# A new order of operations and loads for an attention and mixer kernel

## The chip, the cores and the metric

The kernel runs on one core of one Trainium2 chip. The metric is the device time of one execution in microseconds, as the median of several runs. A core has five engines that run their own instruction streams in order and wait for each other by semaphores: TensorE (PE in the profile; its weight loads are listed apart as PEld), VectorE (DVE), ScalarE (ACT), GpSimd (POOL) and SyncE (SP). Matmul results go to PSUM, which has eight banks here of 128 partitions x 512 floats. POOL issues all loads that change float32 into bfloat16; SP issues stores and transposes by transfer.

## The reference

Eight batches of 576 positions; attention with 8 heads of 64, a causal window of 128 positions and a bias that falls off with distance; then a mixer with two small networks, over positions and over channels:

```python
scores = scale * np.matmul(q, k.transpose(0, 1, 3, 2))
scores = np.where(mask, scores + bias[None], -1e9)      # mask: 0 <= i - j < 128
attn = softmax(scores);  x = attn @ v                   # heads side by side: 8 x 576 x 512
h = np.maximum(x.transpose(0, 2, 1) @ w_tok1, 0.0) @ w_tok2      # 576 -> 256 -> 576
u = x + h.transpose(0, 2, 1)
return u + np.maximum(u @ w_ch1, 0.0) @ w_ch2                    # 512 -> 1536 -> 512
```

Inputs and output are float32; the kernel computes in bfloat16 with float32 sums.

## The kernel before, in words

Batches go in pairs. A pair has nine blocks of 128 positions: four of the even batch (0 to 3), four of the odd one (4 to 7), and block 8, called the tail, which holds the last 64 positions of both batches. The window of 128 means that a block needs the keys and values of itself and of the block before it alone.

For each block the steps are these, with their lines. Load q, k and v (line 518, POOL). Transpose q and k on PE (638) and copy them out of PSUM (644, DVE or ACT); from the tenth block on a transpose by transfer on SP does it (627). Scores (678, PE; two blocks of the first batch, 0 and 1, add the bias on PE in 687). Exponential (701, ACT). Multiplication by the mask (711, DVE; not in blocks 0 and 1). Values (745, PE). Division by the sum (758 and 761, DVE, or 767, ACT). When a batch's blocks are there: the first token matrix (790, then 800 for the last 64 positions), a ReLU (808 or 809), the second token matrix (833, 829 for the tail), the addition (851, or in the first batch 836 on PE and 848 on ACT), and a transposition of the result (868 on PE and 874, or from batch 2 on by transfer, 859). Then the channel network: first matrix (1015, 1030, 1073 for the tail, 952 in the last batch), ReLU (1036, 1078), second matrix (1218, 1118, 1247), with seven products of halves in place of eight, whose sums of operands DVE makes (576 and 594 for weights, 1055 for activations). DVE adds the result (1186), and it is stored.

While PE works on the channel network of a batch, the attention of the next batch is woven in between. At the start there is no such work, so the first batch's attention is a bare chain.

The order of all this is not written out. A planner in the kernel's own Python (class `Plan`, lines 66 to 314) takes every operation with an engine, a cost in ns, a rank and its dependencies, and builds the order of each engine by simulating them at build time: of the operations that could start first, the one with the lowest rank goes. It also has a model of the loads: when the stream of loads begins (`START`), how long each occupies it (packets times `PACKET`), and how long after that its data is there (`LATE`, with a second value for loads issued after `FETCH`). `CASTS` says when the first four float32 tiles are there. POOL issues the loads in the order of the list `LOADS`; at most eight are out at a time. A load of q or k also needs a free buffer of five, and so the transposes of the block that had it before.

In `LOADS`, q2 means q of block 2, and so on; W1 and W2 are the token matrices (P1 a second copy of W1's last rows, T0 the last columns of W2), A0 to A3 are quarters of the first channel matrix (three of its twelve column groups each), and B0 to B3 quarters of the second. Blocks 0 and 3 of q and k are not in the list: they come as float32 by SP and ACT (line 481) and are cast (533).

Where the plan has a gap on PE in the first 60 us, `emit` puts filler matmuls on a tile of zeros (line 1302) there, as long as the planned gap, so that PE is never without work for long. They are fixed instructions: they run whether or not the gap is there.

The random numbers: each part of the program (the first batch's attention, then each batch) had a seed, and each of its operations' ranks was moved by a random amount of up to 1500 ns (`SHIFT`); a seed of 0 leaves a part alone.

Of the kernel before, what the change touches and what calls it, by code (L numbers as in the profile page):

```python
# [3 lines left out]

# [58 lines left out]
    pass  # L63


class Plan:
    def __init__(self):
        self.rings, self.ops, self.orders, self.part = {}, [], 0, 0

    def ring(self, name, slots, pair=None):  # L70
        self.rings[name] = Ring(slots, pair)
# [4 lines left out]
    def op(self, eng, cost, emit, rank, makes=(), adds=(), part=None, uses=(), reads=(), needs=(),  # L76
           after=0.0, order=None, bus=0.0, other=None, mode=0, behind=()):
        def many(x):
            return list(x) if isinstance(x, (list, tuple)) else [x]

        o = Op()
        o.eng, o.cost, o.emit, o.rank, o.after, o.part = eng, cost, emit, rank, after, self.part
        o.t0 = o.done = None
        o.order, o.bus, o.other, o.mode = order, bus, other, mode
        o.n = len(self.ops)
        o.deps = set(many(needs))
        o.behind = list(behind)
# [29 lines left out]

    def run(self):
        ops = self.ops
        dice = [random.Random(x) for x in SEEDS]  # L120
        for o in ops:
            if SEEDS[o.part]:
                o.rank += dice[o.part].uniform(-SHIFT, SHIFT)
        succ = {o: [] for o in ops}
        left, held = {}, []
        ready = {o: o.after for o in ops}
# [21 lines left out]
        todo = len(ops)  # L148
        lines, coming, clock, flying = ([], []), [], START, 0

# [55 lines left out]
        while todo:  # L206
# [94 lines left out]
    def emit(self, spin):  # L301
# [11 lines left out]
        for _, _, go in sorted(work, key=lambda w: w[:2]):  # L313
# [20 lines left out]
RANKH = 0  # L334
RELU = 350
SUMS_AT = 60e3
SEEDS = [45795, 495947, 190309, 331881, 0, 67117, 67408, 179769, 445757]
SHIFT = 1500.0
UNIT_LATE = False
SECOND_LATE = True  # L340
BIASED = [0, 1]
THIRD = [(4, 5)]
# [7 lines left out]
DENSE = 20000.0  # L350
CHILLY = 7400.0
MORE = 150.0
START = 3900.0
RAW = 3
CASTS = [4800.0, 5400.0, 6000.0, 6000.0]
PACKET = 0.813
LATE = (2400.0, 2790.0)
FETCH = 9500.0
STORE = 774.0
TURN = [(792.0, 1267.0), (1380.0, 2400.0)]  # L360
RATES = [(0.37, 0.23), (0.52, 0.35), (0.47, 0.18)]
# [1 line left out]
EARLY = 1  # L363


LOADS = ("q2 k2 k1 q1 v0 W2 k8 q8 v2 v1 v3 v8 W1 q7 k7 A0 P1 k5 q5 k4 v5 "
         "q4 A1 v4 k6 q6 A2 v7 v6 A3 T0 B0 B1 B2 B3")


@with_exitstack  # L370
def kernel(
# [16 lines left out]
    P = nc.NUM_PARTITIONS  # L388
    B, H, S, D = q.shape
# [4 lines left out]
    NC = S // P  # L394
    R = S - NC * P
# [5 lines left out]
    NHT = DCH // P  # L401
# [12 lines left out]
    plan = Plan()  # L414
# [106 lines left out]
    def weights(parts):  # L521
        return [plan.dma(lambda o=o, i=i: nc.gpsimd.dma_start(out=o, in_=i), n, s) for o, i, n, s in parts]

    w1 = moe_w_tok1[0 : NC * P, :].rearrange("(c p) n -> p c n", p=P)
    w2 = moe_w_tok2.rearrange("(j p) s -> p j s", p=P)
    c1 = moe_w_ch1.rearrange("(j p) h -> p j h", p=P)
    c2 = moe_w_ch2.rearrange("(j p) c -> p j c", p=P)

    for i_, raw in enumerate(raws):
        buf, i = block(0, (0, RAW)[i_ // 2])["qk"], i_ % 2  # L530

        def cast(eng=dve_.tensor_copy, raw=raw, buf=buf, i=i):
            eng(out=buf()[:, i, :, :], in_=raw.rearrange("p (h d) -> p h d", h=H))

        plan.op("DVE", (520, 660)[i], cast, -100 + i_, makes=buf, after=CASTS[i_],
                **({"other": ("ACT", 600, lambda cast=cast: cast(act_.copy))} if i_ > 1 else {}))
    if PADT:
        for i in range(2):
            plan.op("DVE", 190, lambda i=i: dve_.memset(W1p[(1 - i) * R : (2 - i) * R, i, :], 0.0), -90)
    lw1, lw2, lw2t, lc1, lc2 = [], [], [], [], []  # L540
    for item in LOADS.split():
        what, n = item[:-1], int(item[-1])
        if what in ("q", "k", "v"):
            load(what, 0, n, parts_of(0, n))
        elif what == "W":
            if n == 1:
                lw1 += weights([(W1[:, 0:NC, :], w1, 512, 2080)] +
                               [(W1p[0:R, 0, :], moe_w_tok1[NC * P : S, :], 64, 210)])
            else:
                lw2 += weights([(W2[:, :, :], w2[:, :, 0 : NC * P], 256, 2630)])  # L550
        elif what == "P":
            lw1 += weights([(W1p[R:P, 1, :], moe_w_tok1[NC * P : S, :], 64, 210)])
        elif what == "T":
            lw2t += weights([(W2t[:, :, :], w2[:, :, NC * P : S], 256, 300)])
        elif what == "A":
            hs = slice(n * DCH // 4, (n + 1) * DCH // 4)
            lc1 += weights([(WC1[:, :, hs], c1[:, :, hs], 512, 2500)]) * (NHT // 4)
        else:
            js = slice(n * NHT // 4, (n + 1) * NHT // 4)
            lc2 += weights([(WC2[:, js, :], c2[:, js, :], 384, 2680)]) * (NHT // 4)  # L560
    for pr in range(1, B // 2):
        for blk in sum(turns_of(pr), []):
            for name in "qkv":
# [358 lines left out]
    def unit(b, u, rank, uT, tt, r2):  # L922
# [23 lines left out]
        def product(m, bk, more=(), new=True):  # L946
            l, r, ws, ts = L[m]

            def go():
                for c in range(2):  # L950
                    for cb in range(2):
# [192 lines left out]
    def second(b, rank, r2, ss, sums, ub):  # L1144
        pr, half = b // 2, b % 2
        final = b == B - 1
        g1, g2, g3 = bank(ANY), bank(TWO if final else ANY), bank(ANY)
        obs = {}
        capt = {}

# [22 lines left out]
        def both(bk):  # L1173
            return bk().rearrange("p (c n) -> p c n", c=2)[:, :, 0:HN]

        def evict(m, bk, row, col, last):
            key = (row, col)
            blks = [half * NC + 2 * row, half * NC + 2 * row + 1]
            cols = slice(col * HN, (col + 1) * HN)
            old = obs.get(key)  # L1180
            ob = old or obs.setdefault(key, plan.buf("ob"))

            def go():
                v = ob().rearrange("p (c n) -> p c n", c=2)
                src = v if old else ub()[:, blks[0] : blks[0] + 2, cols]
                dve_.tensor_tensor(out=v, in0=both(bk), in1=src, op=ALU.add)  # L1186

            rk = rank(0)
# [12 lines left out]
            if late:  # L1201
                plan.dma(store, 2 * P, -1, uses=ob)
            else:
                plan.op("SP", 550, store, rk, uses=[ob])

        DONE = {1: (0, 0, False), 5: (1, 1, False), 6: (0, 1, False), 7: (1, 1, True), 2: (0, 0, True), 3: (0, 1, True), 4: (1, 0, True)}
        for m in PRODUCTS:
# [5 lines left out]
            for g in range(2):  # L1213
# [60 lines left out]
    side(0, along(-1e6, 1.0, 1.0))  # L1274
    for b in range(B):
        n = LEN[b % 2]
        plan.part = b + 1
        marks["wait"] = []
        main(b, along(base, n, n))
        wait = marks["wait"]  # L1280
        if b + 1 < B:
            nb = b + 1
            tot = SIDE[nb // 2 >= HALVED][nb % 2] + 8 * 216 + 216 + (5 if nb % 2 else 4) * (656 if nb < FROM_U else 432)
            if nb > 1:
                tot -= 450 * sum(by_transfer(nb // 2, x) for x in turns_of(nb // 2)[nb % 2])
# [52 lines left out]
```

## Time and profile before

| What | Value |
|---|---|
| Median of 3 runs | 279.0 us (278.68, 279.0, 279.62) |
| Profiled execution, span from first to last instruction | 277.5 us |
| What lies around the span, median less span | 1.5 us |
| Granted TensorE clock | 0.999 |
| Bytes moved by DMA | 38.71 MB, mean 139 GB/s |

The profile is of one execution. A line of a timeline has the start and the length in us, then engine, line of the kernel, operation, output and inputs, and how many instructions are merged in it; in brackets is idle time of the engine just before, and what ended it. In a group the numbers behind the bar are busy time and the mean length of one in ns, then the idle time before. A matmul's length holds its way through the queue, so matmuls overlap, and starts tell more than lengths. A load's row has its size and the time from issue to landing.

### The profile page before, as it was taken

The numbers are of one execution on the slowest core, as the hardware profiler recorded it, in microseconds if no ns is written. First come the engines' busy times: TensorE is split into PE (matmuls) and PEld (weight loads), VectorE is DVE, ScalarE is ACT, GpSimd is POOL, SyncE is SP. The second block draws the span as 40 slices with busy tenths as digits, with TensorE's granted clock in tenths as the row PEclk, the third lists the DMA queues.
The fourth block names the chain that finished last, engine by engine and source line by source line (L and its number), as shares of the span: only waits on it lengthen the run. The fifth ranks groups of instructions, "written<-read, shape, count | busy, mean of one in ns | idle before, by whom it ended". The sixth has DMA issues, their size and how long they took to land.

```text
span 277.5 us, 7005 instructions
## 1 busy us (share of the span) xinstructions
PE 269.9 (97%) x2827; PEld 180.1 (65%) x2827; DVE 209.6 (76%) x497; ACT 139.8 (50%) x238; POOL 114.0 (41%) x144
## 2 busy tenths in 40 slices
PE   7899999999999999999999999999999999999994
PEld 3565765685686555595567655576667645689883
DVE  6577699978897569853989478763989549877983
ACT  5573894336960298207951096206860079105650
POOL 8889865940256037900585009600472220013000
PEclk9999999999999999999999999999999999999999
DMA  8999999999699999999899989999499750043014
GB/s 155 163 159 160 183 194 186 155 133 218 107 113 105 177 234 140 131 135 185 175 134 143 196 214 97 138 155 246 50 120 99 197 140 0 2 127 121 1 57 135
DMA packets 167553, 38.71 MB, mean 139 GB/s; under 512 B 155808, under 2 KB 166688, under 8 KB 167520
## 3 DMA queue, kind: packets, MB, share of 16 engines
q0 software_dynamic: 114032, 19.77, 92.1%
q1 hardware_dynamic: 51264, 17.83, 33.4%
q10 hardware_dynamic: 2224, 0.66, 1.2%
q8 instruction: 22, 0.36, 0.5%
q14 instruction: 11, 0.09, 0.1%
HBM read 35.85 MB, written 9.44 MB: 163 GB/s over the span
## 4 chain that ended last, share of the span: by engine, by line
PE 93%; DMA 2%; DVE 2%; ACT 1%; issue 0%; SPq 0%; DVEq 0%
PE ps L1218 26%; PE ps L1030 25%; PE ps L745 7%; PE ps L678 6%; PE ps L790 5%; PE ps L833 5%; PE ps L1073 4%; PE ps L1118 4%; PE ps L952 3%; DMA raw<-in_q_dram 2%; PE ps L1302 2%; PE ps L638 2%; PE ps L800 1%; PE ps L829 1%; PE ps L868 1%; PE ps L1015 1%
## 5 line engine op out<-in xcount | busy, mean ns | idle before, releaser
L1030 PE MATMUL ps<-uT,WC 128*128 128x512 bf16 x328 | 79.1, 379 | 0.4 <-DVE xb L761 0.4
L701 ACT ACTIVATE pe<-ps 128x1024 bf16<-128x1024 f32 (+1 forms) x76 | 63.5, 889 | 27.0 <-PE ps L678 25.7
L518 POOL DMA_DIRECT2D v<-in_v_dram x40 | 34.1, 857 | 92.7 <-PE ps L745 89.2
L1036 ACT ACTIVATE r<-ps 128x512 bf16<-128x512 f32 x75 | 44.4, 602 | 40.5 <-PE ps L1030 38.5
L1030 PEld LDWEIGHTS <-WC 128*128 128x128 bf16 x328 | 29.3, 98 | 30.1 <-issue 1.3
L711 DVE TENSOR_TENSOR pe<-pe,mask 128x1024 bf16<-128x1024 bf16 (+1 forms) x64 | 38.1, 608 | 7.2 <-ACT pe L701 6.8
L1218 PEld LDWEIGHTS <-r 128*128 128x128 bf16 x372 | 35.9, 98 | 7.2 <-issue 0.2
L518 POOL DMA_DIRECT2D qk<-in_k_dram x38 | 32.8, 870 | 3.6 <-DMA v<-in_v_dram 1.6
L518 POOL DMA_DIRECT2D qk<-in_q_dram x38 | 32.8, 868 | 2.7 <-DMA WC<-in_moe_w_ch_dram 1.0
L1218 PEld LDWEIGHTS <-s 128*128 128x128 bf16 x288 | 27.5, 98 | 6.0 <-issue 1.3
L761 DVE TENSOR_TENSOR xb<-ps,rt 128x256 bf16<-128x256 f32 (+1 forms) x72 | 29.2, 416 | 0.7
L745 PEld LDWEIGHTS <-pe 128*128 128x128 bf16 (+1 forms) x560 | 22.3, 98 | 8.7 <-DVE pe L711 2.2
L745 PE MATMUL ps<-v,pe 128*128 128x65 bf16 (+1 forms) x560 | 26.2, 194 | 0.2 <-DVE pe L711 0.2
L1218 PE MATMUL ps<-WC,r 128*128 128x256 bf16 x192 | 25.4, 273 | 0.0
L1218 PE MATMUL ps<-WT,s 128*128 128x256 bf16 x192 | 24.6, 273 | 0.0
L851 DVE TENSOR_TENSOR ub<-ps,xb 128x512 bf16<-128x512 f32 x34 | 21.2, 681 | 1.8 <-PE ps L833 1.8
L1218 PE MATMUL ps<-WT,r 128*128 128x256 bf16 x180 | 22.4, 272 | 0.0
L678 PEld LDWEIGHTS <-qkT 64*128 64x128 bf16 x560 | 14.7, 94 | 11.1 <-issue 9.4
L1186 DVE TENSOR_TENSOR raw<-ps,ub 128x512 f32<-128x512 f32 x21 | 14.3, 685 | 9.1 <-PE ps L1218 8.9
L678 PE MATMUL ps<-qkT 64*128 64x128 bf16 (+1 forms) x304 | 19.4, 216 | 0.0
L1078 ACT ACTIVATE r2t<-ps 128x512 bf16<-128x512 f32 x12 | 7.2, 603 | 22.5 <-PE ps L1073 22.5
L758 DVE RECIPROCAL rt<-ps 128x4 f32<-128x4 f32 (+1 forms) x76 | 12.4, 174 | 6.8 <-PE ps L745 6.3
(105 smaller groups left out, 350.7 us busy)
## 6 DMA issues: line engine op xcount, KB each, us to landing
out_dram<-raw SPq DMA_DIRECT2D x17, 256.0 KB, 2.6
v<-in_v_dram POOLq DMA_DIRECT2D x32, 128.0 KB, 5.4
qk<-in_q_dram POOLq DMA_DIRECT2D x30, 128.0 KB, 5.6
qk<-in_k_dram POOLq DMA_DIRECT2D x30, 128.0 KB, 5.4
WC<-in_moe_w_ch_dram POOLq DMA_DIRECT2D x8, 384.0 KB, 9.1
out_dram<-ob SPq DMA_DIRECT2D x6, 256.0 KB, 2.6
out_dram<-ob POOLq DMA_DIRECT2D x4, 256.0 KB, 3.1
out_dram<-raw POOLq DMA_DIRECT2D x4, 256.0 KB, 2.9
```

The source lines that it names most:

```text
L518: nc.gpsimd.dma_start(out=to()[p0 : p0 + n, :, :], in_=rows(src, b, s0, n))
L678: pe_.matmul(wide(e)[:, i, kind, a:z], lhsT=ts[kb]()[e * D : (e + 1) * D, NHP + i, :], rhs=ts[blk]()[e * D : (e + 1) * D, i, a:z], start=n ...
L701: act_.activation(out=pb()[:, e, :, lo:, c0:c1_], in_=wide(e)[:, :, lo:, c0:c1_], func=ACT.Exp, scale=scale)
L711: dve_.tensor_tensor(out=o, in0=o, in1=heads(mk, es), op=ALU.mult)
L745: pe_.matmul(view()[a:z, at, i, :], lhsT=pb()[:, e, i, kind, a:z], rhs=vb()[:, h, 0 : D + 1], start=m == 0, stop=m == len(mms) - 1, skip_g ...
L761: dve_.tensor_tensor(out=x4(), in0=view()[r0:r1_, :, :, 0:D], in1=rt()[r0:r1_, 0:n, :, :].broadcast_to([r1_ - r0, n, 4, D]), op=ALU.mult)
L790: pe_.matmul(t1[j]()[:, :], lhsT=W1[:, c, j * P : (j + 1) * P], rhs=xb()[:, blk, :], start=c == 0, stop=False)
L851: plan.op("DVE", 690, lambda blk=blk, ht=ht, hs=hs: dve_.tensor_tensor(out=ub()[:, blk, :], in0=ht()[:, hs], in1=xb()[:, blk, :], op=ALU.a ...
L1030: pe_.matmul(ct()[:, :], lhsT=WC1[:, cb, t * P : (t + 1) * P], rhs=uT()[:, cb, :], start=cb == 0, stop=cb == NCB - 1)
L1036: plan.op("ACT", 600, lambda t=t, ct=ct: act_.activation(out=r2()[:, t, :], in_=ct()[:, :], func=ACT.Relu), rk, part=(r2, t), uses=[ct], o ...
L1186: dve_.tensor_tensor(out=v, in0=both(bk), in1=src, op=ALU.add)
L1218: pe_.matmul(of(bk, c), lhsT=l(t, c), rhs=w(t), start=first, stop=g == 1 and t == HK - 1, skip_group_check=True)
```

## The change

Four things change together, all in what the planner is given.

The model of the first transfers is set to other values: the stream of loads begins 1300 ns later, loads issued after 9.0 us land 3500 ns after their place in the stream instead of 2790 (after 9.5 us), the float32 tiles are there at 5.0, 5.68, 7.56 and 8.04 us, and W1, W2 and the quarters B are given fewer packets. The list of loads has another order. Since A, B and W1's parts no longer come in the order in which they are numbered, the lists of weights (`lw1`, `lc1`, `lc2`) are filled by place. The random shifts come from a hash instead of a generator, and there are now seeds for groups of 30 operations, and of two parts for each batch (its channel network, and the next batch's attention and token mixing).

Two new constants, `EV` and `GONE`, stand at values that change nothing. No operation is added or removed, but the planner may give a copy to another engine and makes other fillers. Some fifteen lines are added ahead of most of the program, so a line such as 833 is 848 in the changed kernel; the text uses the old numbers, and calls the same line there its twin.

```diff
+def offset(o):
+    seed = SEEDS.get(o.group, 0)
+    z, full = (seed << 20) + o.part * 1000 + o.at, (1 << 64) - 1
+    z = (z + 0x9E3779B97F4A7C15) & full
+    z = ((z ^ (z >> 30)) * 0xBF58476D1CE4E5B9) & full
+    z = ((z ^ (z >> 27)) * 0x94D049BB133111EB) & full
+    return ((z ^ (z >> 31)) >> 11) * 2.0**-52 - 1.0 if seed else 0.0
...
+        o.at = self.inside.get(self.part, 0)
+        self.inside[self.part] = o.at + 1
+        o.group = self.part * 10 + min(o.at // GROUP, 9)
...
-        dice = [random.Random(x) for x in SEEDS]
         for o in ops:
-            if SEEDS[o.part]:
-                o.rank += dice[o.part].uniform(-SHIFT, SHIFT)
+            o.rank += SHIFT * offset(o)
...
-SEEDS = [45795, 495947, 190309, 331881, 0, 67117, 67408, 179769, 445757]
+SEEDS = {0: 846071, 4: 412855, 5: 343328, 6: 901394, 7: 671959, 8: 764867, 10: 416701, 11: 351752, 12: 70309, 20: 619675, 21: 120696, 22: 577973, 23: 405716, 30: 213057, 31: 165847, 32: 71954, 40: 404590, 41: 482568, 50: 286568, 51: 611926, 60: 579527, 61: 819459, 62: 379002, 70: 640395, 71: 934419, 72: 439456, 80: 109511, 81: 910233, 82: 748762, 90: 519950, 91: 197367, 101: 150347, 102: 405724, 110: 7956, 111: 36992, 112: 363882, 120: 129293, 122: 874736, 130: 359970, 131: 803027, 140: 23914, 141: 388902, 142: 496852, 150: 220523, 151: 220010, 152: 75231, 153: 900190}
+GROUP = 30
 SHIFT = 1500.0
+EV = 0.0
+GONE = False
...
-START = 3900.0
+START = 5200.0
-CASTS = [4800.0, 5400.0, 6000.0, 6000.0]
+CASTS = [5000.0, 5680.0, 7560.0, 8040.0]
-LATE = (2400.0, 2790.0)
-FETCH = 9500.0
+LATE = (2400.0, 3500.0)
+FETCH = 9000.0
...
-LOADS = ("q2 k2 k1 q1 v0 W2 k8 q8 v2 v1 v3 v8 W1 q7 k7 A0 P1 k5 q5 k4 v5 "
-         "q4 A1 v4 k6 q6 A2 v7 v6 A3 T0 B0 B1 B2 B3")
+LOADS = ("k1 q1 k2 q2 v0 k8 q8 v1 v2 v8 v3 W1 q7 q4 k4 W2 q6 "
+         "k6 A0 k7 q5 A3 k5 v7 v4 A1 v6 v5 A2 B0 T0 P1 B2 B1 B3")
...
-                lw1 += weights([(W1[:, 0:NC, :], w1, 512, 2080)] +
+                lw1[0:2] = weights([(W1[:, 0:NC, :], w1, 512, 1670)] +
...
-                lw2 += weights([(W2[:, :, :], w2[:, :, 0 : NC * P], 256, 2630)])
+                lw2 += weights([(W2[:, :, :], w2[:, :, 0 : NC * P], 256, 1520)])
...
-            lc2 += weights([(WC2[:, js, :], c2[:, js, :], 384, 2680)]) * (NHT // 4)
+            lc2[n * NHT // 4 : (n + 1) * NHT // 4] = weights([(WC2[:, js, :], c2[:, js, :], 384, 2400)]) * (NHT // 4)
...
-        plan.part = b + 1
+        plan.part = 2 * b + 1
...
+            plan.part = 2 * b + 2
```

More of the change, by code (lines that the diff above doesn't have):

```diff
@@ L2 @@
 import math
-import random
 import concourse.bass as bass
@@ L63 @@
     pass
+def offset(o):
[5 more added lines that the diff above has]
+    return ((z ^ (z >> 31)) >> 11) * 2.0**-52 - 1.0 if seed else 0.0
 class Plan:
     def __init__(self):
-        self.rings, self.ops, self.orders, self.part = {}, [], 0, 0
+        self.rings, self.ops, self.orders, self.part, self.inside = {}, [], 0, 0, {}
     def ring(self, name, slots, pair=None):
@@ L539 @@
             plan.op("DVE", 190, lambda i=i: dve_.memset(W1p[(1 - i) * R : (2 - i) * R, i, :], 0.0), -90)
-    lw1, lw2, lw2t, lc1, lc2 = [], [], [], [], []
+    lw1, lw2, lw2t, lc1, lc2 = [None] * 3, [], [], [None] * NHT, [None] * NHT
+    plan.items = []
     for item in LOADS.split():
         what, n = item[:-1], int(item[-1])
+        first = len(plan.ops)
         if what in ("q", "k", "v"):
@@ L546 @@
             if n == 1:
-                lw1 += weights([(W1[:, 0:NC, :], w1, 512, 2080)] +
+                lw1[0:2] = weights([(W1[:, 0:NC, :], w1, 512, 1670)] +
                                [(W1p[0:R, 0, :], moe_w_tok1[NC * P : S, :], 64, 210)])
             else:
-                lw2 += weights([(W2[:, :, :], w2[:, :, 0 : NC * P], 256, 2630)])
+                lw2 += weights([(W2[:, :, :], w2[:, :, 0 : NC * P], 256, 1520)])
         elif what == "P":
-            lw1 += weights([(W1p[R:P, 1, :], moe_w_tok1[NC * P : S, :], 64, 210)])
+            lw1[2:3] = weights([(W1p[R:P, 1, :], moe_w_tok1[NC * P : S, :], 64, 210)])
         elif what == "T":
@@ L556 @@
             hs = slice(n * DCH // 4, (n + 1) * DCH // 4)
-            lc1 += weights([(WC1[:, :, hs], c1[:, :, hs], 512, 2500)]) * (NHT // 4)
+            lc1[n * NHT // 4 : (n + 1) * NHT // 4] = weights([(WC1[:, :, hs], c1[:, :, hs], 512, 2500)]) * (NHT // 4)
         else:
             js = slice(n * NHT // 4, (n + 1) * NHT // 4)
-            lc2 += weights([(WC2[:, js, :], c2[:, js, :], 384, 2680)]) * (NHT // 4)
+            lc2[n * NHT // 4 : (n + 1) * NHT // 4] = weights([(WC2[:, js, :], c2[:, js, :], 384, 2400)]) * (NHT // 4)
+        plan.items.append(plan.ops[first:])
     for pr in range(1, B // 2):
@@ L1146, in second @@
         final = b == B - 1
-        g1, g2, g3 = bank(ANY), bank(TWO if final else ANY), bank(ANY)
+        SB = ANY if final or not GONE else ONE
+        g1, g2, g3 = bank(SB), bank(TWO if final else SB), bank(SB)
         obs = {}
@@ L1186, in go @@
                 dve_.tensor_tensor(out=v, in0=both(bk), in1=src, op=ALU.add)
-            rk = rank(0)
+            rk = rank(0) - EV
             kw = {"adds": ob} if old else {"makes": ob, "reads": [(ub, x) for x in blks]}
```

## The prediction

> **What bounds the kernel now.** I read the page first, then PE's waits, then PE, DVE, ACT and the loads in order of time for the first 30 us.
>
> ```profile
> span 277.5 us, 7005 instructions
> PE 269.9 (97%) x2827; PEld 180.1 (65%) x2827; DVE 209.6 (76%) x497; ACT 139.8 (50%) x238; POOL 114.0 (41%) x144
> PE 93%; DMA 2%; DVE 2%; ACT 1%; issue 0%; SPq 0%; DVEq 0%
> ```
>
> Span, busy time, and the engine shares of the chain that ended last: PE holds 93% of it. So time can only come from PE's work, from its waits, or from what PE does that is no work. The last is there:
>
> ```profile
> L1302 PE MATMUL ps<-zero 128*128 128x452 bf16 (+10 forms) x45 | 11.8, 381 | 1.0 <-DVE zero L482 1.0
> PE ps L638 <- DVE qk L533: 2.0, 3, 1.3
> PE ps L1030 <- DVE xb L761: 0.4, 1, 0.4
> PE ps L745 <- DVE pe L711: 0.2, 1, 0.2
> 50.00:100.00 50.00, 50.00 (x512) 33.39 (x510) 40.02 (x93) 24.17 (x42) 18.34 (x23) 1.00 1.54 149
> 200.00:250.00 50.00, 50.00 (x512) 33.12 (x510) 38.39 (x83) 20.24 (x33) 11.81 (x16) 1.00 0.73 97
> ```
>
> A group of matmuls (busy, mean), PE's waits (us, times, longest), two stretches (length, then busy PE, PEld, DVE, ACT, POOL, granted clock, DMA share, GB/s). The 45 filler matmuls (line 1302) all stand before 25 us; PE is busy with them for up to 11.8 us, a union of overlapping spans that counts their queues double. After 30 us PE waits for 0.6 us in all, and in the late stretches for nothing. Hence the first 25 us are the only place with something to gain, and any wait set up later is a loss.
>
> ```profile
> 6.23 0.40 PE L638 MATMUL ps<-ident,qk 128*128 128x128 bf16 x4 [0.19 <-DVE qk L533]
> 8.31 0.78 PE L638 MATMUL ps<-ident,qk 128*128 128x128 bf16 x8 [1.34 <-DVE qk L533]
> 9.02 0.40 PE L678 MATMUL ps<-qkT 64*128 64x128 bf16 x8
> 11.10 0.23 PE L678 MATMUL ps<-qkT 64*128 64x128 bf16 x2
> 14.05 1.25 PE L1302 MATMUL ps<-zero 128*128 128x508 bf16 x5
> 21.22 0.68 PE L745 MATMUL ps<-v,pe 128*128 128x65 bf16 x16
> 21.82 1.90 PE L790 MATMUL ps<-xb,W 128*128 128x512 bf16 x8
> 23.65 0.60 PE L800 MATMUL ps<-xb,W1p 64*128 64x512 bf16 x2
> 24.98 1.46 PE L833 MATMUL ps<-r,W 128*128 128x512 bf16 x6
> 28.91 0.62 PE L1015 MATMUL ps<-uT,WC 128*128 128x128 bf16 x8
> ...
> 7.53 0.72 DVE L533 CAST qk<-raw 128x512 bf16<-128x512 f32 x1 [1.04 <-DMA raw<-in_q_dram]
> 8.17 0.41 DVE L644 COPY qkT<-ps 128x512 bf16<-128x512 bf16 x1
> 9.12 0.69 DVE L644 COPY qkT<-ps 128x1024 bf16<-128x1024 bf16 x1 [0.55 <-PE ps L638]
> ...
> 9.45 1.08 ACT L701 ACTIVATE pe<-ps 128x512 bf16<-128x512 f32 x2 [0.82 <-PE ps L678]
> 11.77 1.94 ACT L701 ACTIVATE pe<-ps 128x1024 bf16<-128x1024 f32 x2 [1.23 <-PE ps L678]
> 19.00 1.09 ACT L701 ACTIVATE pe<-ps 128x512 bf16<-128x512 f32 x2 [1.10 <-PE ps L745]
> ```
>
> PE, DVE, ACT in order of time (start, length, what). The first batch is a chain of small steps: transpose, copy, scores, exponential, mask, values, then the token weights at 21.82. DVE's second copy of block 0 (8.17) was ready when PE's transposes of 6.23 ended, but stood behind a cast whose input landed at 7.5.
>
> ```profile
> 1.37 1.03 POOL L518 DMA_DIRECT2D qk<-in_q_dram  x1 [0.30 <-issue]
> 5.01 0.91 POOL L518 DMA_DIRECT2D v<-in_v_dram  x1
> 5.87 0.74 POOL L522 DMA_DIRECT2D W<-in_moe_w_tok_dram  x1
> 14.69 0.79 POOL L522 DMA_DIRECT2D W<-in_moe_w_tok_dram  x1
> 17.87 0.88 POOL L518 DMA_DIRECT2D qk<-in_k_dram  x1 [0.94 <-DVE qkT L644]
> 18.74 0.77 POOL L522 DMA_DIRECT2D WC<-in_moe_w_ch_dram  x1
> 36.36 0.76 POOL L522 DMA_DIRECT2D WC<-in_moe_w_ch_dram  x1 [1.22 <-DMA WC<-in_moe_w_ch_dram]
> ...
> qk<-in_q_dram POOLq DMA_DIRECT2D x1, 128.0 KB, 7.1
> v<-in_v_dram POOLq DMA_DIRECT2D x1, 128.0 KB, 6.8
> W<-in_moe_w_tok_dram POOLq DMA_DIRECT2D x1, 256.0 KB, 7.2
> W<-in_moe_w_tok_dram POOLq DMA_DIRECT2D x1, 256.0 KB, 5.9
> qk<-in_k_dram POOLq DMA_DIRECT2D x1, 128.0 KB, 4.5
> WC<-in_moe_w_ch_dram POOLq DMA_DIRECT2D x1, 384.0 KB, 5.6
> WC<-in_moe_w_ch_dram POOLq DMA_DIRECT2D x1, 384.0 KB, 10.7
> ```
>
> Seven loads: when POOL issues each, and, in the same order, its time to landing. Sums: q2 (the first) lands at 8.5, v0 (the fifth) at 11.8, W2 at 13.1, W1 at 20.6, k7 at 22.4, A0 at 24.3, B3 (the last weight) at 47.1. So a load of 128 KB takes (11.8 - 8.5) / 4 = 0.83 us of the stream and W2 some 1.25. The stream is the pace-maker: what moves ahead in it moves all behind it back.
>
> **The change, part by part.** The engines together do the same real work in another order (some copies pass from DVE to ACT or back); the fillers are 42 of 17,868 columns instead of 45 of 18,712. Counted from the first token matmul, PE's columns and its changes between row groups come out alike in both orders, to under 0.05 us. So no gain or loss from PE's work itself: what counts is when the first token matmuls start, and waits behind.
>
> *Block 0.* DVE now does both copies of block 0 before the casts of block 3. Copy two starts when the transposes of 6.23 end (6.65) and takes 0.41; scores of block 0 at 7.1 instead of 9.02. In return both casts of block 3 are DVE's (one was ACT's): 0.72 from 7.53, then 0.6, until 8.85, and block 3's transposes move from 8.31 to 8.9. Nobody needs block 3 early now.
>
> *Load order k1 q1 k2 q2 v0.* Block 1 takes the two slots at 8.5 and 9.3. Its transposes follow block 3's at 9.4, its two bias groups (0.9 us) cover the two copies (0.69 each, DVE, 9.6 to 11.0), and its scores come at 11.0, where block 3's were (11.10). ACT then begins a full block at 11.65 against 11.77, no gain, but its next ones follow without the waits of before: block 2 (landed 10.9, scores at 13.0) 13.6 to 15.5, block 3 (scores at 14.8) 15.5 to 17.5, the tail block 17.5 to 18.6, against 19.00 to 20.09. That is 1.5 us earlier.
>
> *W2 moved behind q4 and k4.* All of k8, q8, v1, v2, v8, v3, W1 land 1.25 us earlier: W1 at 19.3, v3 before it at no later than 18.1. With scores of the tail block ending near 17.2, PE still has, in its new order: values of block 2 (0.5), three fillers (0.5), values of block 3 with two fillers between (0.7), two fillers (0.35), values of the tail with two fillers and two token matmuls between (1.2), six token matmuls (1.3): 4.55 us, so line 800's twin starts at 21.75 against 23.65. Inputs in time: v3 18.1 for a use at 18.2, the tail's masks near 19.1 for 19.3. Gain here 1.9; the bounds are 1.25 (the loads alone) and 2.3 (all waits gone).
>
> *What comes late next: W2.* From line 800 to line 833 the old order took 24.98 - 23.65 = 1.33 us; the new one would be there at 23.1. W2 now stands after all that k7 stood after, less k7, plus q4, k4: 22.4 + 0.83 = 23.2, with bounds 22.9 and 23.9 from the rounding of the rows and the size of the load. Waiting behind it on PE are all eight matmuls of line 833 and everything after. I take 23.4: 1.6 us gained.
>
> *A0 moved back by three loads* (q4, q6, k6 ahead of it and k4 for k7): 24.3 + 3 x 0.83 = 26.8. Line 1015 came 3.93 after line 833, so it would be at 27.35: covered, by 0.5. Next the transposes of block 7 need k7 at 26.8 + 0.83 = 27.65 for a use at 27.8: bare. A3, k5, v4 and v6 have some 0.5 each by the same count. I charge 0.2 for these together (0 to 0.6).
>
> *The last weights.* The set ahead of B3 is the same, so it lands near 47.1 again; the second product that reads it has moved back to about 53, its first neighbours read B0 and B2 alone. No wait. DVE's sums that read B3 (0.47 each, two) stand before the five additions of batch 1 and would be done near 48.1, the first addition is due near 49: cover 0.8.
>
> *After 50 us.* Ranks have new offsets in groups of 30 operations. Counted in columns at full clock, the distance in PE time from a block's scores to its values has, from batch 2 on, the same least values in both orders (1.9 and 2.1 us); from the last line 833 of a batch to its first line 1030 it is 6.1 us at least against 6.5 (batch 2), by transfer; where the old had no wait. Batch 1 alone is tighter, 3.1 against 4.2. I take 0, bounds -0.6 (its waits go) and +1.5. The last 45 matmuls and stores are alike: 0. Code that is added but switched off (`EV`, `GONE`) costs nothing.
>
> **Sum.** -1.6 + 0.2 + 0 = -1.4 us: span 276.1. The median of the runs lies 1.5 above the profiled span (279.0 against 277.5), so 277.6.
>
> [...]
>
> **Rivals.**
>
> *The landings take the gain back.* The order is drawn for the landings of another order. If v1 to v3, W2, A0 and k7 each come 0.5 late, line 833 starts at 23.9 and block 7 costs 0.5 more: 1.1 - 0.2 - 0.5 = 0.4 us gained, 278.6. For it: four uses with under 0.3 us of cover. Against: the stream's pace is steady at 0.83.
>
> *W2 late, slower.* W2 is now needed as soon as it lands; before it lay ready for 11.9 us (13.1 to 24.98). The point that decides is a landing at 25.0. If POOL may issue only when older loads have landed (the 1.22 us it sat before 36.36 shows such a wait), one missed place puts two loads' time and the wait on it: 23.4 + 1.7 + 0.9 = 26.0, all behind shifts 1.0, and A0 and k7 with it: 280.2. Against: its issue would be near 17.8, 5 us ahead.
>
> *A wait in batch 1 or later.* Batch 1's five additions stand in a row on DVE (0.62 each), then copies, and PE comes 1.1 us sooner: a wait of 1 to 1.5 there leaves 279.0.
>
> [...]
>
> **Chances.** Forecast (277.6; its own range 276.5 to 278.4) 0.6. Landings take it back 0.13 and a wait in batch 1 or later 0.09: both mostly within 0.3%. W2 late 0.16, clock 0.02. 0.3% is 0.84 us, about what a measurement of this kernel tells from no change. Faster 0.6, same 0.18, slower 0.22. Range: below, all waits gone, 1.9 + 0.6 = 2.5, 276.5; above, to W2 late, 280.2.
>
> **What would show it.** Right: line 678's twin at 7.1 for block 0, ACT's tail exponentials near 17.5, line 800's twin near 21.8, line 833's near 23.4, 1.5 us kept to the end. Wrong: a PE wait on W2 or A0 of over 1 us, new PE waits after 50 us, or ACT's second full block not following the first.

## The result, and the profile after

The changed kernel takes 277.38 us in the median (277.34 to 277.7), the kernel before 279.22 beside it: a ratio of 0.9945, 95% interval 0.993 to 0.9961. It is faster by 1.84 us; 277.6 was predicted. The median of the kernel before rests on four executions here; all 72 of it on record have 278.88, and against these the gain is 1.5 us, which is also what the ratio says (1.1 to 2.0). The profiled execution took 277.36, with a span of 275.6 against 277.5; the spans of 68 other executions of the kernel before have a median of 277.1. Three executions of the kernels in the experiments ran far longer than the others of the same kernel (284.87, 959.72 and 351.16 us), and medians and ratios are without them.

The page of the changed kernel: span, busy times, engine shares of the chain that ended last.

```profile
span 275.6 us, 6968 instructions
...
PE 268.4 (97%) x2790; PEld 180.8 (66%) x2824; DVE 210.3 (76%) x496; ACT 139.1 (50%) x239; POOL 114.0 (41%) x144
...
PE 81%; DMA 6%; DVE 5%; POOL 4%; issue 2%; SPq 1%; POOLq 0%
```

All waits of its PE (us, times, longest):

```profile
PE ps L1319 <- DVE zero L494: 1.0, 1, 1.0
PE ps L1045 <- DMA uT<-ub: 0.2, 1, 0.2
```

Its fillers (line 1302 is 1319 there), as a group with busy time and mean length behind the bar:

```profile
L1319 PE MATMUL ps<-zero 128*128 128x460 bf16 (+13 forms) x42 | 12.1, 401 | 1.0 <-DVE zero L494 1.0
```

Behind the start one wait of 0.2 us is left. The fillers are 42 as foreseen; of PE's 2824 matmuls 34 have no record in this trace. In the chain DMA, DVE and POOL now hold 15%: the loads themselves have become part of what sets the end. PE, then ACT and POOL of the changed kernel in order of time (start, length):

```profile
7.33 0.40 PE L693 MATMUL ps<-qkT 64*128 64x128 bf16 x8
9.51 1.04 PE L702 MATMUL ps<-WS 128*128 128x256 bf16 x8
10.61 0.23 PE L693 MATMUL ps<-qkT 64*128 64x128 bf16 x2
13.42 0.61 PE L653 MATMUL ps<-ident,qk 128*128 128x128 bf16 x8
21.68 0.60 PE L815 MATMUL ps<-xb,W1p 64*128 64x512 bf16 x2
23.01 0.59 PE L848 MATMUL ps<-r,W 128*128 128x512 bf16 x2
27.05 0.62 PE L1030 MATMUL ps<-uT,WC 128*128 128x128 bf16 x8
27.50 0.83 PE L653 MATMUL ps<-ident,qk 128*128 128x128 bf16 x8
...
11.27 1.94 ACT L716 ACTIVATE pe<-ps 128x1024 bf16<-128x1024 f32 x2 [2.43 <-PE ps L693]
13.39 4.83 ACT L716 ACTIVATE pe<-ps 128x1024 bf16<-128x1024 f32 x6 [0.18 <-PE ps L693]
...
13.47 0.78 POOL L534 DMA_DIRECT2D W<-in_moe_w_tok_dram  x1
17.42 0.74 POOL L534 DMA_DIRECT2D W<-in_moe_w_tok_dram  x1
19.89 0.81 POOL L534 DMA_DIRECT2D WC<-in_moe_w_ch_dram  x1
20.63 0.95 POOL L530 DMA_DIRECT2D qk<-in_k_dram  x1
```

The last four rows issue W1, W2, A0 and k7; the loads' own view has, in the same order, their time to landing:

```profile
W<-in_moe_w_tok_dram POOLq DMA_DIRECT2D x1, 256.0 KB, 5.3
W<-in_moe_w_tok_dram POOLq DMA_DIRECT2D x1, 256.0 KB, 5.5
WC<-in_moe_w_ch_dram POOLq DMA_DIRECT2D x1, 384.0 KB, 7.1
qk<-in_k_dram POOLq DMA_DIRECT2D x1, 128.0 KB, 7.3
```

W1 landed at 18.8 (20.6 before), W2 at 22.9, A0 at 27.0, k7 at 27.9. Line 815 starts at 21.68 (its twin 800 at 23.65), line 848 at 23.01 (833 at 24.98), line 1030 at 27.05 (1015 at 28.91). So the changed kernel is 1.97 us ahead at line 848, and it ends 1.9 ahead. From the first start of line 848 to the end of the span the changed kernel takes 275.6 - 23.01 = 252.6 us, the old kernel 277.5 - 24.98 = 252.5. The whole gain is made before 23 us and kept. W2 landed 0.09 us before it was used, A0 0.05.

### The profile page after: what moved, and what is told of

It is laid out like the page before. It is cut to its first block, busy times and chain, and to the rows that moved or that the text cites. A ratio compares the mean times of both kernels' runs of the same rounds, so it can differ in the third digit from the quotient of the medians.

```text
span 275.6 us, 6968 instructions
## 1 busy us (share of the span) xinstructions
PE 268.4 (97%) x2790; PEld 180.8 (66%) x2824; DVE 210.3 (76%) x496; ACT 139.1 (50%) x239; POOL 114.0 (41%) x144
## 4 chain that ended last, share of the span: by engine, by line
PE 81%; DMA 6%; DVE 5%; POOL 4%; issue 2%; SPq 1%; POOLq 0%
PE ps L1234 25%; PE ps L1045 24%; PE ps L760 6%; PE ps L693 5%; DMA qk<-in_k_dram 5%; PE ps L805 4%; PE ps L848 4%; PE ps L1088 4%; PE ps L967 3%; PE ps L1133 3%; DVE pe L726 2%; POOL qk L530 2%; POOL v L530 1%; DMA uT<-ub 1%; PE ps L815 1%
## 5 line engine op out<-in xcount | busy, mean ns | idle before, releaser
L1045 PE MATMUL ps<-uT,WC 128*128 128x512 bf16 x306 | 77.9, 379 | 1.3 <-DMA uT<-ub 0.2
L716 ACT ACTIVATE pe<-ps 128x1024 bf16<-128x1024 f32 (+1 forms) x76 | 63.4, 890 | 19.1 <-PE ps L693 18.8
L1051 ACT ACTIVATE r<-ps 128x512 bf16<-128x512 f32 x77 | 45.0, 604 | 51.4 <-PE ps L1045 49.3
L726 DVE TENSOR_TENSOR pe<-pe,mask 128x1024 bf16<-128x1024 bf16 (+1 forms) x64 | 38.7, 609 | 12.0 <-ACT pe L716 11.5
L760 PEld LDWEIGHTS <-pe 128*128 128x128 bf16 (+1 forms) x560 | 22.6, 98 | 9.1 <-DVE pe L726 1.3
L760 PE MATMUL ps<-v,pe 128*128 128x65 bf16 (+1 forms) x560 | 26.9, 194 | 0.3
L1202 DVE TENSOR_TENSOR raw<-ps,ub 128x512 f32<-128x512 f32 x22 | 15.0, 686 | 8.1 <-PE ps L1234 8.1
L1093 ACT ACTIVATE r2t<-ps 128x512 bf16<-128x512 f32 x12 | 7.2, 600 | 22.9 <-PE ps L1088 22.7
```

Of the source, the lines that this page charges most:

```text
L716: act_.activation(out=pb()[:, e, :, lo:, c0:c1_], in_=wide(e)[:, :, lo:, c0:c1_], func=ACT.Exp, scale=scale)
L726: dve_.tensor_tensor(out=o, in0=o, in1=heads(mk, es), op=ALU.mult)
L760: pe_.matmul(view()[a:z, at, i, :], lhsT=pb()[:, e, i, kind, a:z], rhs=vb()[:, h, 0 : D + 1], start=m == 0, stop=m == len(mms) - 1, skip_g ...
L1045: pe_.matmul(ct()[:, :], lhsT=WC1[:, cb, t * P : (t + 1) * P], rhs=uT()[:, cb, :], start=cb == 0, stop=cb == NCB - 1)
L1051: plan.op("ACT", 600, lambda t=t, ct=ct: act_.activation(out=r2()[:, t, :], in_=ct()[:, :], func=ACT.Relu), rk, part=(r2, t), uses=[ct], o ...
```

## The experiments

The theories at the start were these. Theory 1: the gain is the 1.25 us that W2 no longer takes from the loads ahead of it. Theory 2: it is the new model of the first transfers, which gives DVE another order at block 0 and fillers that fit. Theory 3: it is the new random offsets. The table has every kernel that ran: its median, the ratio with its interval to the kernel before, which ran beside each (medians 278.84 to 279.22), and, from the profile, the span, the first start of line 848 (or 833), and the difference of the two, here called the rest.

| Kernel | Median us | Ratio | Span | 848 | Rest |
|---|---|---|---|---|---|
| before | 278.8 to 279.2 | | 277.5 | 24.98 | 252.5 |
| changed | 277.38 | 0.9945 (0.993 to 0.9961) | 275.6 | 23.01 | 252.6 |
| loads alone | 279.15 | 1.0008 (0.9999 to 1.0017) | 277.7 | 24.38 | 253.3 |
| model alone | 287.63 | 1.0309 (1.0273 to 1.0345) | 287.2 | 24.32 | 262.9 |
| no offsets | 279.25 | 1.0007 (0.9993 to 1.0021) | 277.2 | 24.19 | 253.0 |
| old loads | 290.91 | 1.0437 (1.0405 to 1.0469) | 288.4 | 23.82 | 264.6 |
| W2 issued sixth | 278.66 | 0.9996 (0.9983 to 1.0009) | | 24.51 | |
| W2 issued later | 279.11 | 1.0021 (1.0 to 1.0043) | 277.5 | 24.57 | 252.9 |
| cast first | 277.54 | 0.9956 (0.9943 to 0.9969) | 275.8 | 23.84 | 252.0 |
| no fillers | 279.97 | 1.0042 (1.0027 to 1.0058) | 278.8 | 24.00 | 254.8 |
| start's offsets alone | 278.08 | 0.9964 (0.9943 to 0.9986) | 276.2 | 23.10 | 253.1 |
| later offsets alone | 278.66 | 0.999 (0.9969 to 1.0011) | 276.8 | 23.85 | 253.0 |
| fillers to 12 us | 278.91 | 0.9987 (0.996 to 1.0014) | 275.9 | 22.68 | 253.2 |
| other offsets | 290.25 | 1.038 (1.031 to 1.0451) | 286.8 | 23.98 | 262.8 |

### One part alone, or one part left out

*Loads alone*: the old kernel with the new list of loads (and its lists of weights filled by place, as in the change).

```diff
-LOADS = ("q2 k2 k1 q1 v0 W2 k8 q8 v2 v1 v3 v8 W1 q7 k7 A0 P1 k5 q5 k4 v5 "
-         "q4 A1 v4 k6 q6 A2 v7 v6 A3 T0 B0 B1 B2 B3")
+LOADS = ("k1 q1 k2 q2 v0 k8 q8 v1 v2 v8 v3 W1 q7 q4 k4 W2 q6 "
+         "k6 A0 k7 q5 A3 k5 v7 v4 A1 v6 v5 A2 B0 T0 P1 B2 B1 B3")
```

> The kernel before with the new list of loads alone: old values in the model of the transfers, old seeds. Theory 1 (the gain is W2's 1.25 us taken out of the way of the first batch's loads): most of the gain, 278.0, and line 790 near 20.6. Theory 2 (the gain is the model's: DVE's order at block 0 and fillers that fit): no gain, 279.2. Theory 3 (the gain is the new seeds): 279.2 too.

*Model alone*: the old kernel with the new values of the model.

```diff
-START = 3900.0
+START = 5200.0
-CASTS = [4800.0, 5400.0, 6000.0, 6000.0]
+CASTS = [5000.0, 5680.0, 7560.0, 8040.0]
-LATE = (2400.0, 2790.0)
-FETCH = 9500.0
+LATE = (2400.0, 3500.0)
+FETCH = 9000.0
...
-                lw2 += weights([(W2[:, :, :], w2[:, :, 0 : NC * P], 256, 2630)])
+                lw2 += weights([(W2[:, :, :], w2[:, :, 0 : NC * P], 256, 1520)])
```

(and W1's and the B quarters' values, as in the change)

> The kernel before with the new values of the model alone (START, CASTS, LATE, FETCH, packets of W1, W2 and B): old list of loads, old seeds. Theory 1: 279.2, since W2 still stands in the way. Theory 2: block 0's scores near 7.1 and 278.0. Theory 3: 279.2.

*No offsets*: the changed kernel without any random offset, its list of seeds empty.

```diff
+SEEDS = {}
```

> The changed kernel without any random shift of ranks. Theories 1 and 2: the start keeps its gain, 277.6 to 278.0, if the plain ranks make no new waits. Theory 3: the gain goes, 279.2 or more.

*Old loads*: the changed kernel with the list of loads of before (the first diff, reversed).

> The changed kernel with the old list of loads, planned anew for it: new model, new seeds. Theory 1: the first token matmuls come 1.25 us later than with the new list, 278.6. Theory 2: 277.6. Theory 3: 277.6.

No part holds the gain. At line 848 the loads alone are worth 0.6 us, the model alone 0.66, both without offsets 0.79, all three 1.97. What each gains at the start is lost again behind 25 us or nearly so. Without offsets 0.5 goes in the rest, and the time outside the span is 1.9 to 2.0 us, where it is 1.7 to 1.9 in the other kernels. The loads alone lose 0.8 in the rest. Of their two new waits of PE

```profile
PE ps L745 <- ACT xb L767: 0.9, 1, 0.9
PE ps L1030 <- DMA uT<-ub: 0.5, 1, 0.5
```

(columns as above) the first stands at 17.23, ahead of line 833, and takes from the gain at the start; the second, at 95.40, is 0.5 of the 0.8, and 0.3 has no place. The model alone loses far more. Its waits of PE:

```profile
PE ps L1030 <- DMA uT<-ub: 4.2, 1, 4.2
PE ps L745 <- DVE pe L711: 1.6, 3, 1.1
...
PE ps L1247 <- DVE ob L1186: 0.8, 1, 0.8
```

The longest of them is in batch 2. Its place on PE, and SP's queue ahead of it, in order of time:

```profile
101.56 1.87 PE L1030 MATMUL ps<-uT,WC 128*128 128x512 bf16 x4 [4.22 <-DMA uT<-ub]
...
91.95 2.57 SPq L859 DMA_TRANSPOSE uT<-ub  x2
94.62 0.54 SPq L1198 DMA_DIRECT2D out_dram<-raw  x1
95.85 1.19 SPq L1135 DMA_DIRECT2D out_dram<-raw  x2
97.08 2.59 SPq L859 DMA_TRANSPOSE uT<-ub  x2
```

Three stores stand on SP between the second and the third of the four transposes of `uT`. In the kernel before, and in the changed one, the four go out in a row:

```profile
87.88 5.41 SPq L859 DMA_TRANSPOSE uT<-ub  x4
```

```profile
85.83 6.00 SPq L874 DMA_TRANSPOSE uT<-ub  x4
```

Two stretches of the model alone around that wait (length, busy times of the five engines, then the granted clock, third from the end):

```profile
98.00:102.00 4.00, 0.43 (x2) 0.19 (x3) 0.09 (x1) 0.00 (x0) 0.00 (x0) 0.73 1.03 263
102.00:104.00 2.00, 2.00 (x6) 0.68 (x5) 0.00 (x0) 0.48 (x1) 0.00 (x0) 0.50 0.96 183
```

In the wait of 4.22 us PE's clock falls to half (0.50), from 99.8 us to 106.6. Of that PE works 5.0 us, from 101.56 on, which by estimate costs some 2.5 us more. The waits after line 833 come to 7.5 us with two smaller ones (0.7 on a load of q, 0.2), so 10 of the 10.4 us by which this kernel's rest is longer have a place.

The changed kernel with the old list of loads has a rest 12 us longer than the changed kernel's. PE's waits hold 9.0 of it, the longest of them

```profile
PE ps L760 <- DVE pe L726: 3.4, 7, 1.2
PE ps L967 <- DVE tt L931: 1.6, 1, 1.6
PE ps L1045 <- issue: 1.4, 1, 1.4
PE ps L1088 <- DMA uTt<-ub: 1.3, 1, 1.3
```

and in one stretch, after three of these waits within 3.2 us (1.15, 0.19 and 1.25), the clock falls too, which makes 1.7 us:

```profile
130.00:140.00 10.00, 8.75 (x78) 5.97 (x79) 2.25 (x4) 5.00 (x8) 0.00 (x0) 0.83 0.97 171
```

The other 1.3 was not split.

### W2's place in the stream

Both kernels keep the changed kernel's order on PE, DVE, ACT and SP. Only POOL issues W2 at another place:

```diff
+    ISSUED = ("k1 q1 k2 q2 v0 W2 k8 q8 v1 v2 v8 v3 W1 q7 q4 k4 q6 k6 A0 k7 q5 A3 k5 v7 v4 A1 v6 v5 A2 B0 T0 P1 B2 B1 B3").split()
...
+    at = dict(zip(LOADS.split(), plan.items))
+    flat = [o for x in ISSUED for o in at[x]]
+    for o, t in zip(flat, sorted(o.t0 for o in flat)):
+        o.t0 = t
...
```

for W2 sixth, and for W2 later

```diff
+    ISSUED = ("k1 q1 k2 q2 v0 k8 q8 v1 v2 v8 v3 W1 q7 q4 k4 q6 k6 W2 A0 k7 q5 A3 k5 v7 v4 A1 v6 v5 A2 B0 T0 P1 B2 B1 B3").split()
...
```

> The plan of the changed kernel, every engine's order as it is; only POOL issues W2 as the sixth load again instead of the sixteenth. Theory 1 (the way of W2 is the gain): k8 to v3 land some 1.25 us later (W1 near 20.0), and the second token matrix (line 848) starts 1.0 +- 0.3 us later, near 24.0; time 278.4. Theory 2 (the loads have slack, the gain is PE's and DVE's new order): 848 moves by less than 0.3 us; 277.4.

> The plan of the changed kernel, only W2 is issued after q6 and k6, two places later; it then lands near 24.6 instead of 22.9, q6 and k6 near 23.1 and 23.9. My step 'what comes late next: W2' says that PE waits for it at line 848: start at 24.6 instead of 23.0, a wait of 1.6 us in PE's list of waits, and 279.0 us. Rival (other waits lie in its shadow, as the A0 and k7 that follow are bare too): 848 late, but block 7 and line 1030 no later than before by the same amount, 278.0 or less.

With W2 sixth the median is 1.28 us longer, as theory 1 had it, and beside its own runs of the kernel before nothing clear of noise is left of the gain (0.9996). The profiled execution of this kernel had its clock at 0.95 from 8 us on, so its span is left out of the table and only PE's starts are read:

```profile
14.81 0.61 PE L653 MATMUL ps<-ident,qk 128*128 128x128 bf16 x8 [0.98 <-DMA qk<-in_q_dram]
24.51 0.62 PE L848 MATMUL ps<-r,W 128*128 128x512 bf16 x2
```

The tail block's transposes, at 13.42 in the changed kernel, wait 0.98 us for q8 and start at 14.81, 1.39 late; q8 itself lands 1.38 later (14.67 against 13.29), and POOL waits for loads alone before it issues it, not for PE. Line 848 is 1.5 late (1.0 was expected, at full clock). So the delay enters at the loads behind W2 and stays to the end. W2's place is worth most of the gain, 1.3 us, but only in this order of operations: with the old model and offsets the whole new list was worth nothing.

With W2 issued later PE waits for it, here in order of time:

```profile
24.57 0.61 PE L848 MATMUL ps<-r,W 128*128 128x512 bf16 x2 [1.35 <-DMA W<-in_moe_w_tok_dram]
```

24.57 was the expected 24.6, and 279.11 the expected 279.0. Nothing of the 1.56 us comes back later; the rest is 0.3 longer. W2 is the next bound, at once.

### Block 0's copies

```diff
+    dve = sorted((o for o in plan.ops if o.eng == "DVE"), key=lambda o: o.t0)
+    dve[4].t0 = dve[3].t0 - 0.5
```

The fifth operation of DVE, the cast of block 3's q, goes ahead of the fourth, block 0's second copy.

> The plan of the changed kernel, only DVE casts block 3's q before it makes the second copy of block 0, as the kernel before did. If my step on block 0 is right in all its parts, the scores of block 0 come 1.2 to 1.7 us later (near 8.7 instead of 7.33), ACT's first full block comes no later than 11.65 since block 1's loads set it, and the time stays at 277.4. Rival (the start of ACT's work is what pulled the rest forward): line 848 some 1 us later, 278.4.

PE of this kernel in order of time:

```profile
8.21 0.40 PE L693 MATMUL ps<-qkT 64*128 64x128 bf16 x8 [1.10 <-DVE qkT L659]
23.84 0.59 PE L848 MATMUL ps<-r,W 128*128 128x512 bf16 x2
```

The time is that of the first expectation, 277.54, and the way is that of the rival: ACT's first full block starts at 12.16 (no later than 11.65 was expected, 11.27 in the changed kernel), and line 848 does come 0.83 us later. The rest is 0.6 shorter than the changed kernel's, so most of it is given back. What is lost shrinks to 0.5 by the second batch's token matrix (44.8 against 44.3), since the changed kernel loses 0.3 where A0 and k7 land and this one does not: from line 848 to 1030 it takes 4.04 us, this one 3.92, and the eight transposes behind it take 0.68, here 0.45. By the fourth batch's token matrix 0.16 is left (110.25 against 110.09). In between lies the one wait that the changed kernel has there, for a transpose of `uT`:

```profile
93.01 1.02 PE L1045 MATMUL ps<-uT,WC 128*128 128x512 bf16 x4 [0.17 <-DMA uT<-ub]
```

So of what is gained before line 848, the last part is worth little: the next transfers take it.

### The fillers

```diff
-FILL = 60000.0
+FILL = 0.0
```

in the kernel without fillers, and `FILL = 12000.0` in the one with fillers up to 12 us.

> The changed kernel without its 42 filler matmuls, all else as it is. If the fillers only stand in gaps: 277.4 +- 0.3 with a granted clock of 1.0. If the clock goes down without them: granted clock well below 1 in the first 10 us and for some us after the waits near 8 to 13, real matmuls there twice as long; 278.5 to 281. If fillers overran their gaps: line 848 some 0.5 us earlier (not earlier than W2's landing near 22.9), 276.9.

> The changed kernel with its fillers up to 12 us only (without fillers at all the matmuls ran at half speed up to 12.4 us, and it cost 2.6). If work of PE alone keeps it at full speed from there, with gaps of at most 0.7 us: matmuls of full speed all the way (0.056 us a pair of scores of 128 columns each), 277.4 +- 0.3. If fillers are needed to the end of the gaps: half speed again between 12 and 20 us, 278.5. If fillers overran their gaps: line 848 earlier, but not before W2 at 22.9, 277.3.

Without fillers, PE in order of time:

```profile
10.03 1.91 PE L702 MATMUL ps<-WS 128*128 128x256 bf16 x8
```

and the stretch before 12 us (columns as in the stretches above):

```profile
8.00:12.00 4.00, 3.85 (x28) 2.60 (x30) 1.77 (x3) 1.08 (x2) 3.13 (x4) 1.00 2.42 154
```

The eight bias matmuls take 1.91 us where the changed kernel's took 1.04 (line 702 at 9.51). Matmul starts lie at twice their distance up to 12.5 us (0.11 us from one pair of scores of 128 columns to the next at 12.06 to 12.49, 0.055 in the changed kernel from 10.68 on), and line 848 is 1.0 late. The clock expectation holds in its price, 2.6 us in the median. Its first half is wrong: the granted clock of the stretch reads 1.00 all the same. That column does not show the slow start, though it shows 0.50 after a wait (the model alone, above). The rest is 2.2 longer than the changed kernel's, 1.8 of it in two waits of PE:

```profile
PE ps L1045 <- issue: 1.0, 1, 1.0
...
PE ps L967 <- DVE tt L931: 0.8, 1, 0.8
```

With fillers up to 12 us the pairs of scores between 12 and 15 us keep their 0.055 us, and from there to line 848 groups of the same matmuls take what they take in the changed kernel, to 0.1 us, across gaps of up to 0.7 us between starts (15.46 to 16.16); in the profiled execution line 848 starts at 22.68, as W2 lands (22.6). That gains 0.33 us and does not last: in the last batch PE waits 0.8 us for DVE's sums, and DVE for a transpose,

```profile
249.13 0.76 DVE L931 TENSOR_TENSOR tt<-uT 128x512 bf16<-128x512 bf16 x2 [2.32 <-DMA uT<-ub]
```

where the changed kernel has

```profile
248.01 0.76 DVE L931 TENSOR_TENSOR tt<-uT 128x512 bf16<-128x512 bf16 x2 [0.61 <-DMA uT<-ub]
```

The last of these transposes landed 1.1 us later, though the first was issued 0.6 earlier (239.81 against 240.40): the first took 3.8 us to landing instead of 2.3, with no load or store beside it in either kernel. The median, 278.91, is another matter: ten executions lie between 277.70 and 280.17, and the profiled one is the fastest. The kernel without fillers spreads by 1.5 us too, the changed one, over four executions, by 0.36. So the fillers after 12 us cost nothing on the path that this profile shows, and yet without them the median is 1.5 us longer. What differs between these executions was not seen and stays open; the time at which PE comes to full speed (last section) is a candidate that one trace of each kernel cannot test.

### The random offsets

```diff
+SEEDS = {0: 846071, 4: 412855, 5: 343328, 6: 901394, 7: 671959, 8: 764867}
```

are the start's offsets alone; the later offsets alone are all the others. In the kernel with other offsets

```diff
-    seed = SEEDS.get(o.group, 0)
+    seed = SEEDS.get(o.group, 0) and SEEDS[o.group] + 1
```

> The changed kernel with the random offsets of the first batch's attention alone (groups 0 to 8); all later operations have none. PE's order is that of the changed kernel to beyond 50 us. If the gain of the change is in its start (as my sum says: 1.6 by line 848, 0 after 50 us, for any offsets there): 848 at 23.0 and 277.4. If the offsets of the later parts are what keeps the gain: 848 at 23.0, then losses of 1 us or more behind 50 us, at PE's waits or changes between row groups; 278.2 or more.

> The changed kernel with the offsets of the first batch's attention taken out and all others kept. Model and loads are those of the changed kernel. If loads and model make the start: 848 near 23.0 to 23.3, 277.5. If the first batch's offsets are a part of it (with no offsets at all 848 came at 24.19): 848 near 24.2, and 278.5 if the later orders stay good, 279.2 if they, being drawn after another start, have waits of their own.

> The changed kernel with each seed raised by one, so other random offsets of the same size in the same groups; model and loads as they are. If offsets matter little (my sum has 0, bounds -0.6 and +1.5 for all behind 50 us): 277.4 to 278.9. If the order has to fit to 0.5 us at each batch: 848 between 23 and 24.3, and PE waits of over 1 us for transfers or copies at several batches, 280 to 290 as in the two kernels whose offsets were drawn for another model or other loads.

The start's offsets alone bring line 848 to 23.10, where the changed kernel has it (23.01), and keep 278.08. That lies between the two expectations, 277.4 and 278.2. The later ones alone leave it at 23.85, and 278.66, near the second expectation. So with the new loads and model the start's offsets are worth 1.2 us (from 279.25), the later ones 0.6; together 1.87. The 0.6 is not clear of noise, since the intervals of no offsets (0.9993 to 1.0021) and of the later ones alone (0.9969 to 1.0011) overlap. With the start's offsets alone PE has one wait of note, on a transpose in batch 3 (us, times, longest):

```profile
PE ps L1045 <- DMA uT<-ub: 1.1, 1, 1.1
```

Other offsets of the same size cost 13 us, with these waits of PE:

```profile
PE ps L760 <- DVE pe L726: 3.9, 5, 1.3
PE ps L1234 <- DVE raw L1202: 1.6, 2, 0.8
```

These, one more of 0.8 and two of 0.6 are 7.5 of the 10.2 us by which its rest is longer; where the other 2.7 lie was not split. So none of the three theories holds by itself. W2's place is needed (1.28 us without it) and the offsets are (1.87 without them), each with the other parts in place; what the new loads and offsets would do under the old model was not run.

## Why the prediction was right, point by point

*What bounds the kernel.* Right: the first 25 us were the only place with something to gain, and all of it was gained there. What other orders lost behind 25 us they lost for the most part in waits of PE, and in the half clock (0.50 in the model alone) that came with some of these.

*Block 0.* Scores came at 7.33 instead of the predicted 7.1. In this execution PE came to full speed at 6.3 only; in "W2 issued later", with the same order on PE and full speed from 5.7, they came at 7.14. That block 0's copy comes first is worth 0.83 us at line 848: without it block 0's scores are 0.88 late, and block 3's transposes (9.50 against 8.61) and block 1's scores (11.49 against 10.61) move back with them. So block 1's scores are not set by the loads alone, as the step had it. But 0.67 of the 0.83 comes back by the fourth batch, so in the time it is worth little. Whether block 3 is needed early was not tried by itself.

*Load order.* Right in kind, a little short in size: block 1's scores at 10.61 (11.0 predicted), ACT's first full block at 11.27 (11.65), and the rest of ACT's work follows without a wait longer than 0.18, as was said. Some 0.3 of this is chance: the first load landed at 8.16 in this execution and at 8.43 in the profiled one of before, and between 8.11 and 8.48 in the others.

*W2 moved.* Right. W1 at 18.8 (19.3 predicted), line 815 at 21.68 (21.75), and undoing this alone costs 1.28 us (the step's lower bound was 1.25).

*What comes late next: W2.* The landing was right (22.9; 23.2 with bounds 22.9 and 23.9), the charge was not: 0.3 us was charged for waiting, and W2 came 0.09 before its use. This is the mis-sized term: the step measured 0 instead of 0.3, so 1.97 was gained here instead of 1.6. That it is the bound was right, as W2 issued two places later shows.

W2's 5.5 us from issue to landing here are fewer than the 7.2 of before.

*A0 and k7.* Right in kind, wrong in one cover: A0 at 27.0 (26.8) was used at 27.05, so the 0.5 of cover that was counted for it was not there, and it cost the 0.1 that the comparison with "cast first" shows; k7 at 27.9 (27.65), and the transposes that need it take 0.83 from 27.50 on, where such a group takes 0.61 (at 13.42): 0.2. Together 0.3 against the 0.2 charged.

*After 50 us.* Right, 0: the rest is 252.6 against 252.5. In part that is a balance: the old kernel's two waits of PE behind line 833 (0.17 at 41.5 us, 0.40 at 44.3) are gone, and the 0.3 at A0 and k7 and 0.17 at a transpose have come. The way there, counting the least distances in the order, says only that this order has the same cover as the old one. The offsets that were changed by one show how little would do: 13 us. The bound of +1.5 us was sound for an order that can be read before it runs, not for any order that the planner makes.

*The sum.* -1.4 predicted, -1.9 measured between the two profiled spans, -1.84 between the medians, -1.5 against all executions of the kernel before. Between the two profiles 0.4 of the difference lies at line 848 (W2's charge, and the stream's early start) and 0.1 behind it. But 0.4 is also what the profiled execution of before is longer than the median span of that kernel, 277.1, so the sum may be nearer than it looks. That 277.6 was met this closely is in part luck: the sum starts from that long span, and the 1.5 us added to it, the median of three executions less the span of another, is too short: time less span is 1.76 in the changed kernel and 1.72 to 1.85 in those of before. The two errors largely cancel.

*The rivals.* Landings that take the gain back: not so, W2, A0 and k7 came at -0.3 to +0.25 of their predicted times. W2 late: not so, though W2 issued later is that rival with 1.56 us in place of 2.6. A wait in batch 1 or later: 0.2 in all here, but such waits make most of what the model alone and the old loads lose, and a part of what the loads alone do. The clock, that is, a wait that brings half speed: not here; no wait passes 1.0 us, and the granted clock is 1.00. In the model alone the clock fell to 0.50 in the wait of 4.22 us, and a wait of 1.35 us (W2 issued later) left it at 1.00. In the old loads it had fallen at 130.96 us, the end of 3.2 us of which 2.6 were waits, none of them longer than 1.25: 32 matmuls of line 1088 take 3.34 us from there, where 16 of them take 0.90 at 153.56. No run shows one length of wait at which the clock falls.

## What to carry to other kernels

Where a start is bound by its loads, take the load that is needed last out of the way of the others and move it back until its landing just meets its use; after that it is the bound itself, and another two places cost their full time (1.56 us at line 848 here). A transfer order, a model of landings and an order of operations drawn from it belong together: tried one by one, they were worth nothing or did harm. And count the cover of every load and transpose behind the change in advance: a single transpose took back 0.5 us in the loads alone and 1.1 in the start's offsets alone.

## What the runs showed of the hardware

PE reaches full speed at a time that differs from one profiled execution to another, each of another kernel. With fillers from 1.0 us on, the distance of matmul starts halves at 4.1 us in the kernel before, at 5.7 in "W2 issued later", at 6.3 in the changed kernel and near 6.9 with no offsets; without fillers at 12.5. The records of the granted clock begin at that step in the traces of the kernel before and the changed one (4.1, 6.3), and the column reads 1.00 ahead of it. What sets the time of the step was not tested. Where half speed came back later, it lasted 6.8 us in the model alone (99.8 to 106.6) and by estimate 3.4 us in the old loads, from the mean clock of 0.83 over the 10 us from 130 us on.

Landings are not evenly spaced: in the changed kernel a load of 128 KB lands some 0.85 us after the one before it, until between the tenth transfer and the eleventh (v1 at 14.13, v2 at 16.00) 1.9 us pass, and then 0.25 to 0.85 again. In the kernel before such a step stands between the same places (14.83, 17.30), though the loads there are others; but in "cast first", whose list is that of the changed kernel, it stands between the eleventh and the twelfth (15.22, 16.89), and without fillers between the sixteenth and the seventeenth (18.46, 20.21). What makes it is open.

In the changed kernel a transpose of `uT` by transfer takes 2.3 us from issue to landing when no load or store is under way beside it (118.97 us, 241.68), and 2.9 to 6.5 with five or more of them (85.83 to 178.23). Loads and stores are not all of it, as the 3.8 us in the last batch with fillers to 12 us shows.
